# Attention with v in three pieces of 336, 352 and 336 queries across key steps, instead of 256, 256 and 512

## The chip, the cores and the metric

The kernel runs on one core of a Trainium2 chip, as one program in one launch. The metric is the device time of that core in microseconds (us); lower is better. The engines of the core work side by side, each through its own instructions in order: TensorE (PE in the profile, its weight loads PEld), VectorE (DVE), ScalarE (ACT), GpSimd (POOL) and SyncE (SP), which issues the DMAs. They meet at semaphores.

## What is computed

A transformer block of 2048 tokens of width 576, modulated by a condition vector `c`: multi-query attention of 32 heads of 18, all with one k and one v, and then a channel MLP of width 4608. Cut to the part that the change touches:

```python
def _A_ref(x, wq, wk, wv, wo):
    q = (x @ wq).reshape(B, S, H, Dh).transpose(0, 2, 1, 3)
    k = x @ wk
    v = x @ wv
    scores = jnp.einsum("bhqd,bkd->bhqk", q, k) * (Dh ** -0.5)
    p = softmax(scores, axis=-1)
    o = jnp.einsum("bhqk,bkd->bhqd", p, v)
    return o.transpose(0, 2, 1, 3).reshape(B, S, H * Dh) @ wo
```

Everything is float32; products with matrices that are used often are split into high and low parts.

## The kernel before

The program has three stages: norms, projections and the first softmax maxima; then the attention loop; then the output projection's rest and the MLP. The change is in the attention loop alone.

**Quads and key steps.** The loop goes over 32 quads (`n`): 512 queries (`TB`) of four heads at a time. For each quad the 2048 keys are taken in 16 key steps of 128 keys (`kc`). A key step makes four score products (`st_mm`, L793), one for each head: 128 keys by 512 queries, into one of four psB buffers. ACT takes the exponential of each (L795) into the tile `P` of the key step, which holds 4 x 512 columns. There are three buffers for `P`. The four products with v (`pv_mm`, L782), one for each head, then add V of these 128 keys times `P` into the quad's accumulator psC. They use 32 columns of PE's array each and stand side by side in it. psC has one buffer; when a quad is done, ACT copies it out (`O`, L613), and only then the next quad's products with v may begin.

**Maxima.** The softmax subtracts each query's maximum over the keys, and this is worked out one quad ahead. A unit (`UNITS`, eight to a quad) gives the maxima of 128 queries of two heads (`mx_mm`). For the first head of the pair there are four products of 512 keys each (tokens `m0`), for the second head two (`m1`); each goes into one of three psM buffers, and VectorE reduces it to a maximum (L815). The rest of the second head takes the two tokens `x1` and `r1`: `x1` (L803) multiplies the queries with the difference of two blocks of keys, into a psB buffer, and ACT takes its positive part (`xc`, L806); `r1` multiplies with the other block, into a psM buffer, and VectorE adds `xc` and takes the maximum in one instruction (L813).

**The order by hand.** The loop `for d in range(8 * NQT)` does two key steps each (called a double step here), `n, kd = divmod(d, 8)`. Within it the order of PE's work is a list of tokens. `MIX` is used where a unit of maxima falls on the double step (246 of 256), `PLAIN` in the last ten. `s0` and `s1` are score products on the lower and upper 64 rows of PE's array, and `m0`, `m1`, `x1`, `r1` are as above on rows 0 to 63 or 64 to 127, so that a 0 and a 1 next to each other can run side by side. `P` is a full set of four products with v over 512 queries, and `H` is half a set, over 256. With

```python
    MIX = "x1 m0 m0 s1 s0 r1 H s1 s0 m1 s0 H m0 s1 m1 s0 s1 m0 P".split()
```

the two halves are of the second key step of the double step before, and the `P` is the first key step of this one.

After the second `H`, and after the `P`, the loop calls `between`. It takes the steps of the work beside the loop: the copy and scaling of a finished quad (`post_quad`), loads of the next queries, and, from generators, the modulation products, the output projection of finished blocks (`wo_block`, L594), the second layer norm (`ln2_block`) and, on GpSimd, the splitting of the MLP's weights (`weight_parts`). The schedule is the code's order on each engine; nothing moves an instruction.

Of the kernel before, what the change touches and what calls it, by code (L numbers as in the profile page):

```python
# [14 lines left out]
S, D, H, DH, F = 2048, 576, 32, 18, 4608  # L15
NB = 4
TB = S // NB
# [3 lines left out]
NQT = NB * NQ  # L21
# [11 lines left out]
def block_kernel(ctx: ExitStack, tc, x, wqkv, wo, w1, b1, w2, b2, c, wmod, ident_in, out):  # L33
# [20 lines left out]
    def psC(): return PS["t"].tile([128, 512], F32, name="psC", bufs=1)  # L54

    open_ps("1", 3)
    def big(): return per.tile([128, 10, 512], F32R, name="big", bufs=3)
# [244 lines left out]
    def load_q(n):  # L302
        tb, qd = divmod(n, NQ)
        if n not in QST:
            new_q(n)
        q = QST[n]
        for g in range(2):
            for r in range(3):
                src = qscr[tb, r // 2, 4 * DH * qd:4 * DH * (qd + 1), :]
                src = src.rearrange("(p g d) t -> g d p t", p=2, g=2)[g]  # L310
                sy.dma_start(q[64 * g + DH * r:64 * g + DH * (r + 1)].bitcast(F32), src)
# [30 lines left out]
    def smax_fin1(n):  # L342
        m = MR[n] = pa.tile([128, 16], F32, name="mxf", bufs=2)
        mm = MX.pop(n)
        if n == 0:
            ve.tensor_reduce(m, mm, axis=AX.X, op=ALU.max)
        else:
            ve.tensor_reduce(m[:, :8], mm[:, :8, :], axis=AX.X, op=ALU.max)
            ve.tensor_reduce(m[:, 8:], mm[:, 8:, :3], axis=AX.X, op=ALU.max)

    def smax_fin2(n):
        p = psB()
        pe.transpose(p[:16, :128], MR.pop(n), ident)
        ms = pa.tile([16, 2, 128], F32R, name="ms")
        ac.activation(ms[:, 0], p[:16, :128], AF.Copy, scale=-1.0)
        ve.scalar_tensor_tensor(ms[:, 1], p[:16, :128], -1.0, ms[:, 0].bitcast(F32), op0=ALU.mult, op1=ALU.subtract)
        for g in range(2):
            for s in range(2):
                r = 64 * g + R3 + s
                sy.dma_start(QST[n][r:r + 1].rearrange("o p (t c) -> o (p t) c", c=128).bitcast(F32),  # L360
                             ms[8 * g:8 * (g + 1), s].bitcast(F32))
# [80 lines left out]
    for tb in range(NB):  # L442
# [3 lines left out]
        for i, m in enumerate((4, 0, 1, 2, 3)):  # L446
            np_ = NPART[tb][i]
# [29 lines left out]
            if tb < 2:  # L477
                for _ in range(NSTAT[tb][i]):
                    ln1_stats(*stats.popleft())
                for _ in range(NAPPLY[tb][i]):  # L480
                    b, t = applies.popleft()
# [89 lines left out]
    def ln2_block(tb):  # L571
        if "b" not in B2:
            B2["b"] = b2_scaled(load_b2())
        if tb % 2 == 0:
            YR[tb // 2] = per.tile([128, 2 * KD, TB], F32, name="yr", tag="big", bufs=3)
        for t in range(NT):
            yield from ln2_tile(tb, t)
        if tb % 2:
            R = YR[tb // 2]
            po.tensor_tensor(R[:, 5:7], R[:, 7:9], R[:, 5:7], op=ALU.subtract)  # L580
            yield
            po.tensor_tensor(R[:, 5:7], R[:, 5:7], R[:, 0:2], op=ALU.add)
            yield
# [16 lines left out]
    def wo_block(tb):  # L600
        for t in range(NT):
            for h2 in range(2):
                p = psB()
                wo_mm(tb, t, h2, p, 0, KD)
                wo_add(tb, t, h2, p)
                yield

    def post_quad(n, PV):

        tb, qd = divmod(n, NQ)  # L610
        e = po if n < NQT - 1 else ve
        O = px.tile([128, TB], F32, name="O")
        ac.activation(O, PV, AF.Copy)  # L613
        yield
        yield
        T = px.tile([128, 16, 32], F32, name="T")
        ve.transpose(T.rearrange("p a b -> p (a b)"), O)
        yield
        R = px.tile([128, 16], F32, name="R", bufs=2)
        ve.reciprocal(R, T[:, :, DH])  # L620
        e.tensor_tensor(T, T, R[:, :, None].to_broadcast([128, 16, 32]), op=ALU.mult)
        yield
        if e is po:
            yield
        ve.transpose(O, T.rearrange("p a b -> p (a b)"))
        yield
        A = ATT[tb].rearrange("p (s k) t -> p s k t", s=2)
        if qd == NQ - 1:
            os = A[:, :, KD - 1, :]
        else:  # L630
            os = px.tile([128, 2, TB], F32R, name="os")
        ac.activation(os[:, 0], O, AF.Copy)
        e.tensor_tensor(os[:, 1], O, os[:, 0].bitcast(F32), op=ALU.subtract)
        if qd < NQ - 1:
            for j in range(4):
                k, r = divmod(4 * qd + j, HC)
                sy.dma_start(A[DH * r:DH * (r + 1), :, k, :].bitcast(F32), os[32 * j:32 * j + DH].bitcast(F32))
        yield
# [8 lines left out]
    def load_w1(i, what, save=False):  # L647
        for w in what.split():
            a = 4 * OPS.index(w) if w in OPS else 28
            b = min(a + 4, 31)  # L650
            ends = W1["r"][:, a:b].bitcast(F32), w1scr[i, :, a:b]
            sy.dma_start(*(ends[::-1] if save else ends))
# [99 lines left out]


    SH = 2
    MIX = "x1 m0 m0 s1 s0 r1 H s1 s0 m1 s0 H m0 s1 m1 s0 s1 m0 P".split()
    PLAIN = "s0 s1 s0 s1 P s0 s1 s0 s1 P".split()
    P, PVt = {}, {}
    posts = []
    fill = deque([late_weights()])

    def step(q):
        if q:
            try:
                next(q[0])
            except StopIteration:
                q.popleft()

    units = {}
# [3 lines left out]
                units[8 * (n - 1) + u - SH] = (n, u)  # L772
    assert min(units) == 0 and u1 == 2 * SH

    def pv_mm(n, kc, h0, h1):

        if kc == 0 and h0 == 0:
            PVt[n] = psC()
        t = P.pop((n, kc)) if h1 == 4 else P[n, kc]
        cs = slice(128 * h0, 128 * h1)  # L780
        for j in range(4):
            pe.matmul(PVt[n][32 * j:32 * (j + 1), cs], V[:, kc, :], t[:, j, cs],  # L782
                      start=(kc == 0 and h0 == 0), stop=(kc == 15), skip_group_check=True)
        if kc == 15 and h1 == 4:
            gen = post_quad(n, PVt.pop(n))
            next(gen)
            posts.append(gen)

    def st_mm(n, kc, g, i):
        if (n, kc) not in P:  # L790
            P[n, kc] = pb.tile([128, 4, TB], F32, name="P", bufs=3)
        t = psB()
        pe.matmul(t, KS[64 * g:64 * g + 64, 128 * kc:128 * (kc + 1)], QST[n][64 * g:64 * g + 64, i, :],  # L793
                  start=True, stop=True)
        ac.activation(P[n, kc][:, 2 * i + g, :], t, AF.Exp, scale=SCALE)  # L795
# [21 lines left out]
    def between(n, kc):  # L817

        if kc == 12 and n + 1 < NQT:
            smax_fin1(n + 1)  # L820
        if kc == 13 and n + 1 < NQT:
            smax_fin2(n + 1)
        for gen in list(posts):
            if next(gen, 0) == 0:
                posts.remove(gen)
        if kc == 1 and n >= 1 and n + 2 < NQT:
            load_q(n + 2)
        if kc == 8 and n % NQ == 0 and n:
            fill.append(wo_block(n // NQ - 1))
            if n // NQ - 1 < 2:  # L830
                fill.append(ln2_block(n // NQ - 1))
        if kc % 2:
            step(fill)
        if n > 2 and kc not in (11, 12):
            step(prep)
        if kc == 8 and n == NQT - 1:
            while prep:
                step(prep)
            W1["r"] = per.tile([128, 40, 128], F32R, name="w1a", tag="big", bufs=3)
            load_w1(0, " ".join(OPS) + " tails")  # L840

    for d in range(8 * NQT):
        n, kd = divmod(d, 8)
        if kd == 0 and n % NQ == 0:
            ATT[n // NQ] = big()
        un = units.get(d)
        ns, nm, np_ = [0, 0], [0, 0], 0
        for tok in MIX if un else PLAIN:
            if tok in "PH":
                s, h0 = 2 * d + np_ // 4, np_ % 4  # L850
                np_ += 4 if tok == "P" else 2
                if s:
                    pv_mm(*divmod(s - 1, 16), h0, (np_ - 1) % 4 + 1)
                if np_ % 4 == 0:
                    between(n, s % 16)
                continue
            g = int(tok[1])
            if tok[0] == "s":
                st_mm(n, 2 * kd + ns[g] // 2, g, ns[g] % 2)
                ns[g] += 1  # L860
            else:
                mx_mm(*un, tok[0], g, nm[g])
                nm[g] += tok[0] == "m"
    pv_mm(NQT - 1, 15, 0, 4)
    while fill:
        step(fill)
    a2.__exit__(None, None, None)
# [471 lines left out]
```

## Time and profile before

| | us |
|---|---|
| three runs, median (lowest to highest) | 2322.13 (2321.21 to 2322.68) |
| the profiled execution, first to last instruction | 2317.3 |
| first to last double step with a unit of maxima, start to start | 137.7 to 1381.8 |
| busy in 150 to 1390 us: PE, DVE, ACT, POOL | 1225.69, 1142.13, 1151.64, 545.57 |

The granted TensorE clock averages 0.999 over the span. The page of the profile gives no time of the profiled execution beyond its span. A row of the groups has the line, engine, operation, tiles and shapes, the count, then the busy time, the mean length of one in ns, and the idle time of the engine just before these instructions with what ended most of it. A row of the timeline has start, length, engine, line, operation and tiles, the count of merged instructions, and in brackets the idle time before it. `x8` on a row of the products with v are eight instructions for four products.

### The profile page before, as it was taken

The numbers are of one execution on the slowest core, as the hardware profiler recorded it, in microseconds if no ns is written. First come the engines' busy times: TensorE is split into PE (matmuls) and PEld (weight loads), VectorE is DVE, ScalarE is ACT, GpSimd is POOL, SyncE is SP. The second block draws the span as 40 slices with busy tenths as digits, with TensorE's granted clock in tenths as the row PEclk, the third lists the DMA queues.
The fourth block names the chain that finished last, engine by engine and source line by source line (L and its number), as shares of the span: only waits on it lengthen the run. The fifth ranks groups of instructions, "written<-read, shape, count | busy, mean of one in ns | idle before, by whom it ended". The sixth has DMA issues, their size and how long they took to land.

```text
span 2317.3 us, 44805 instructions
## 1 busy us (share of the span) xinstructions
PE 2279.1 (98%) x16390; PEld 1417.5 (61%) x16390; DVE 1881.2 (81%) x3356; ACT 1655.6 (71%) x3166; POOL 1278.2 (55%) x1491
## 2 busy tenths in 40 slices
PE   8999999999999999999999999999999999999999
PEld 5643334454444454444444435899999988888888
DVE  6589999979999979999889993666666677878786
ACT  5568999979999979999889997444444454444443
POOL 6501534335565416656334332488888767777776
PEclk9999999999999999999999999999999999999999
DMA  6412122212222212222212222444434456666663
GB/s 224 143 62 73 50 77 78 84 45 86 73 76 70 79 50 78 76 73 80 67 60 77 79 73 85 147 150 168 163 139 174 154 171 188 181 177 181 177 180 118
DMA packets 145629, 259.93 MB, mean 112 GB/s; under 512 B 15756, under 2 KB 56588, under 8 KB 145410
## 3 DMA queue, kind: packets, MB, share of 16 engines
q1 hardware_dynamic: 145409, 257.07, 35.0%
q8 instruction: 129, 2.11, 0.4%
q14 instruction: 91, 0.74, 0.1%
HBM read 156.11 MB, written 92.01 MB: 107 GB/s over the span
## 4 chain that ended last, share of the span: by engine, by line
PE 86%; ACT 4%; POOL 2%; DVE 1%; issue 1%; DMA 0%; SPq 0%; POOLq 0%; DVEq 0%; ACTq 0%
PE psC L782 22%; PE psB L1009 16%; PE psB L793 11%; PE psM L315 10%; PE psA L1126 9%; PE psA L1095 8%; PE psB L803 4%; PE psB L594 2%; ACT P L795 2%; ACT O L613 1%; PE psA L594 1%; PE psB L152 0%; PE psB L244 0%; PE psB L199 0%; DMA bigw<-in_wo 0%
## 5 line engine op out<-in xcount | busy, mean ns | idle before, releaser
L795 ACT ACTIVATE P<-psB 128x512 f32<-128x512 f32 x2048 | 1048.1, 619 | 3.1 <-PE psB L793 2.0
L815 DVE TENSOR_REDUCE mx<-psM 128x1 f32<-128x512 f32 x1476 | 943.3, 682 | 47.7 <-PE psM L315 26.3
L782 PE MATMUL psC<-P,V 128*32 128x256 f32 (+1 forms) x6056 | 598.0, 466 | 13.3 <-ACT O L613 13.3
L793 PE MATMUL psB<-qst,KS 64*128 64x512 f32 x2048 | 597.7, 433 | 0.8 <-ACT xc L806 0.8
L315 PE MATMUL psM<-KS,qst 64*128 64x512 f32 x1722 | 596.1, 432 | 0.2
L793 PEld LDWEIGHTS psB<-qst,KS 64*128 64x128 f32 x2048 | 301.5, 184 | 169.1 <-issue 71.7
L1009 PE MATMUL psB<-ops,w1a 128*128 128x512 f32 x1512 | 391.3, 396 | 3.2 <-DVE gx L1031 2.6
L315 PEld LDWEIGHTS psM<-KS,qst 64*128 64x128 f32 x1722 | 284.4, 184 | 122.9 <-DVE mx L813 90.6
L1009 PEld LDWEIGHTS psB<-ops,w1a 128*128 128x128 f32 x1512 | 271.4, 188 | 52.0 <-DVE gx L1031 3.5
L782 PEld LDWEIGHTS psC<-P,V 128*32 128x32 f32 x6056 | 119.5, 108 | 233.4 <-issue 209.3
L1126 PE MATMUL psA<-w2s,big 128*128 128x288 f32 x1488 | 255.4, 295 | 0.0
L1126 PEld LDWEIGHTS psA<-w2s,big 128*128 128x128 f32 x1488 | 221.3, 188 | 6.6
L806 ACT ACTIVATE xc<-psB 128x512 f32<-128x512 f32 x246 | 149.0, 606 | 89.7 <-PE psM L315 75.3
L1029 ACT ACTIVATE psB<-gs 128x512 f32<-128x512 f32 x144 | 86.7, 602 | 124.8 <-DVE gs L1028 124.8
L813 DVE CUSTOM_DVE_ANT_0 xc<-psM,xc 128x512 f32<-128x512 f32 x246 | 167.2, 680 | 1.2 <-ACT xc L806 1.2
L132 POOL MEMSET qst<- 32x1024 f32 x62 | 58.7, 946 | 196.8 <-issue 71.7
L1130 DVE TENSOR_TENSOR XT<-psA,XT 128x576 f32<-128x576 f32 x152 | 113.2, 748 | 48.2 <-PE psA L1126 48.1
L803 PEld LDWEIGHTS psB<-KD,qst 64*128 64x128 f32 x246 | 45.1, 183 | 158.6 <-ACT P L795 108.7
L1033 ACT ACTIVATE big<-gx 128x512 fp32r<-128x512 f32 x72 | 45.6, 633 | 126.0 <-DVE gx L1031 126.0
L1034 POOL TENSOR_TENSOR big<-gx,big 128x512 fp32r<-128x512 f32 x72 | 96.3, 1338 | 68.6 <-ACT big L1033 68.3
L1101 DVE TENSOR_TENSOR XT<-psA,XT 128x576 f32<-128x576 f32 x170 | 125.3, 754 | 5.1 <-PE psA L1095 0.5
L803 PE MATMUL psB<-KD,qst 64*128 64x512 f32 x246 | 122.3, 497 | 0.0
(199 smaller groups left out, 3318.1 us busy)
## 6 DMA issues: line engine op xcount, KB each, us to landing
w1a<-w1scr SPq DMA_DIRECT2D x154, 256.0 KB
w1scr<-w1a SPq DMA_DIRECT2D x98, 256.0 KB
w2scr<-r SPq DMA_DIRECT2D x72, 288.0 KB
w2sum<-r SPq DMA_DIRECT2D x68, 288.0 KB
w2s<-w2sum SPq DMA_DIRECT2D x68, 288.0 KB
w2s<-w2scr SPq DMA_DIRECT2D x29, 576.0 KB
qst<-qscr SPq DMA_DIRECT2D x192, 72.0 KB
w2s<-w2scr SPq DMA_DIRECT2D x34, 288.0 KB
```

Source lines behind the costliest of these rows:

```text
L315: pe.matmul(o, QST[n][64 * g:64 * g + 64, p, 128 * qt:128 * (qt + 1)], KS[64 * g:64 * g + 64, 512 * kb:512 * (kb + 1)], start=True, stop=True)
L782: pe.matmul(PVt[n][32 * j:32 * (j + 1), cs], V[:, kc, :], t[:, j, cs], start=(kc == 0 and h0 == 0), stop=(kc == 15), skip_group_check=True)
L793: pe.matmul(t, KS[64 * g:64 * g + 64, 128 * kc:128 * (kc + 1)], QST[n][64 * g:64 * g + 64, i, :], start=True, stop=True)
L795: ac.activation(P[n, kc][:, 2 * i + g, :], t, AF.Exp, scale=SCALE)
L803: pe.matmul(t, QST[n][64 * g:64 * g + 64, p, 128 * qt:128 * (qt + 1)], KD1[64 * g:64 * g + 64, :], start=True, stop=True)
L806: ac.activation(XC[-1], t, AF.Relu)
L813: ve.tensor_tensor_reduce(c, t, c, 1.0, -3.0e38, ALU.add, ALU.max, o)
L815: ve.tensor_reduce(o, t, axis=AX.X, op=ALU.max)
L1009: pe.matmul(o, x, y, start=(first and i == 0), stop=(i == len(terms) - 1), skip_group_check=True)
L1095: pe.matmul(p[:, i, :288], x[:, ts_], W2S[k][:, y], start=(bool(first) and q == 0), stop=(q == 2), skip_group_check=True)
L1101: ve.tensor_tensor(o, p[:, :, :288], o, op=ALU.add)
L1126: pe.matmul(p[:, nn, :288], x, y, start=(q == 0), stop=(q == len(terms) - 1))
```

## The change

A double step with a unit has three pieces of products with v as before, in the same places of the token list, but of nearly equal width. A constant `CUT = 160, 336` gives the borders. The first piece takes the last 176 queries of the first key step of the double step before and the first 160 queries of its second key step. The second piece takes that key step's other 352 queries. The third takes the first 336 queries of this double step's first key step. `between` is called behind the second and the third piece, as before. In `PLAIN` the two pieces stay 512 wide, but for the rest of 176 in the first of them. The first argument in a piece counts key steps from the double step's first.

```diff
-    MIX = "x1 m0 m0 s1 s0 r1 H s1 s0 m1 s0 H m0 s1 m1 s0 s1 m0 P".split()
+    MIX = "x1 m0 m0 s1 s0 r1 P s1 s0 m1 s0 P m0 s1 m1 s0 s1 m0 P".split()
     PLAIN = "s0 s1 s0 s1 P s0 s1 s0 s1 P".split()
+    CUT = 160, 336
...
-    def pv_mm(n, kc, h0, h1):
-
-        if kc == 0 and h0 == 0:
+    def pv_mm(n, kc, c0, c1):
+
+        if kc == 0 and c0 == 0:
             PVt[n] = psC()
-        t = P.pop((n, kc)) if h1 == 4 else P[n, kc]
-        cs = slice(128 * h0, 128 * h1)
+        t = P.pop((n, kc)) if c1 == TB else P[n, kc]
+        cs = slice(c0, c1)
         for j in range(4):
             pe.matmul(PVt[n][32 * j:32 * (j + 1), cs], V[:, kc, :], t[:, j, cs],
-                      start=(kc == 0 and h0 == 0), stop=(kc == 15), skip_group_check=True)
-        if kc == 15 and h1 == 4:
+                      start=(kc == 0 and c0 == 0), stop=(kc == 15), skip_group_check=True)
+        if kc == 15 and c1 == TB:
...
-        ns, nm, np_ = [0, 0], [0, 0], 0
+        ns, nm = [0, 0], [0, 0]
+        a, b = CUT
+        if un:
+            pieces = [[(-2, b, TB), (-1, 0, a)], [(-1, a, TB)], [(0, 0, b)]]
+        else:
+            pieces = [([(-2, b, TB)] if d - 1 in units else []) + [(-1, 0, TB)], [(0, 0, TB)]]
         for tok in MIX if un else PLAIN:
-            if tok in "PH":
-                s, h0 = 2 * d + np_ // 4, np_ % 4
-                np_ += 4 if tok == "P" else 2
-                if s:
-                    pv_mm(*divmod(s - 1, 16), h0, (np_ - 1) % 4 + 1)
-                if np_ % 4 == 0:
-                    between(n, s % 16)
+            if tok == "P":
+                for s, c0, c1 in pieces.pop(0):
+                    if 2 * d + s >= 0:
+                        pv_mm(*divmod(2 * d + s, 16), c0, c1)
+                if len(pieces) < 2:
+                    between(n, 2 * kd + 1 - len(pieces))
                 continue
...
-    pv_mm(NQT - 1, 15, 0, 4)
+    pv_mm(NQT - 1, 15, 0, TB)
```

## The prediction

> **What bounds the kernel now.** I read the page first, for the stretch that the change touches and for the engines' load in it.
>
> ```profile
> PE   8999999999999999999999999999999999999999
> ...
> DVE  6589999979999979999889993666666677878786
> ACT  5568999979999979999889997444444454444443
> ...
> L795 ACT ACTIVATE P<-psB 128x512 f32<-128x512 f32 x2048 | 1048.1, 619 | 3.1 <-PE psB L793 2.0
> L815 DVE TENSOR_REDUCE mx<-psM 128x1 f32<-128x512 f32 x1476 | 943.3, 682 | 47.7 <-PE psM L315 26.3
> L782 PE MATMUL psC<-P,V 128*32 128x256 f32 (+1 forms) x6056 | 598.0, 466 | 13.3 <-ACT O L613 13.3
> ...
> L315 PEld LDWEIGHTS psM<-KS,qst 64*128 64x128 f32 x1722 | 284.4, 184 | 122.9 <-DVE mx L813 90.6
> ...
> L806 ACT ACTIVATE xc<-psB 128x512 f32<-128x512 f32 x246 | 149.0, 606 | 89.7 <-PE psM L315 75.3
> L813 DVE CUSTOM_DVE_ANT_0 xc<-psM,xc 128x512 f32<-128x512 f32 x246 | 167.2, 680 | 1.2 <-ACT xc L806 1.2
> ```
>
> In the attention loop (about slices 3 to 24 of 40) three engines are nearly full at once, so the shares don't say which one sets the pace. PE's 98% is the weakest of them: ends of matmuls are modelled, and a PE that waits with two products in flight counts as busy. Starts of weight loads show the waiting better. The list of the line that opens a double step says how many there are:
>
> ```profile
> L803 PE MATMUL psB<-KD,qst x246: 491/496/792, 137.7 to 1381.8; 64*128 64x512 f32 x123
> ```
>
> So 245 distances between first and last: (1381.8 - 137.7) / 245 = 5.08 us per double step ("step" below). In code order a step has an opening group (x1 m0 m0 s1 s0 r1), piece 1 of the products with v, a middle group (s1 s0 m1 s0), piece 2, a closing group (m0 s1 m1 s0 s1 m0) and piece 3. The timeline of three such steps, weight loads only, one row for the start of each part, and s0 and r1 of the second opening group (714.02, 714.26):
>
> ```profile
> 709.07 0.18 PEld L803 LDWEIGHTS psB<-KD,qst 64*128 64x128 f32 x1 [0.84 <-issue]
> ...
> 709.98 0.16 PEld L782 LDWEIGHTS psC<-P,V 128*32 128x32 f32 x8 [0.36 <-issue]
> ...
> 710.55 0.19 PEld L793 LDWEIGHTS psB<-qst,KS 64*128 64x128 f32 x2 [0.41 <-issue]
> ...
> 711.22 0.16 PEld L782 LDWEIGHTS psC<-P,V 128*32 128x32 f32 x8 [0.27 <-issue]
> ...
> 711.79 0.18 PEld L315 LDWEIGHTS psM<-KS,qst 64*128 64x128 f32 x1 [0.41 <-DVE mx L813]
> ...
> 712.68 0.16 PEld L782 LDWEIGHTS psC<-P,V 128*32 128x32 f32 x8 [0.26 <-issue]
> ...
> 713.68 0.18 PEld L803 LDWEIGHTS psB<-KD,qst 64*128 64x128 f32 x1 [0.84 <-ACT P L795]
> ...
> 714.02 0.18 PEld L793 LDWEIGHTS psB<-qst,KS 64*128 64x128 f32 x1
> ...
> 714.26 0.18 PEld L315 LDWEIGHTS psM<-KS,qst 64*128 64x128 f32 x1
> ...
> 714.68 0.16 PEld L782 LDWEIGHTS psC<-P,V 128*32 128x32 f32 x8 [0.24 <-issue]
> ...
> 715.25 0.19 PEld L793 LDWEIGHTS psB<-qst,KS 64*128 64x128 f32 x2 [0.41 <-issue]
> ...
> 715.92 0.16 PEld L782 LDWEIGHTS psC<-P,V 128*32 128x32 f32 x8 [0.36 <-issue]
> ...
> 716.49 0.18 PEld L315 LDWEIGHTS psM<-KS,qst 64*128 64x128 f32 x1 [0.41 <-DVE mx L813]
> ```
>
> Differences of starts: opening group 0.91 (709.07 to 709.98), piece 1 0.57, middle group 0.67, piece 2 0.57, closing group 0.89, piece 3 1.00, sum 4.61: PE's own work. In the next step the opening group takes 1.00 instead (713.68 to 714.68). The 0.41 or 0.84 idle in front of the loads behind a piece is the piece itself streaming. The row at 711.79 names L813, but the first row below shows that L813 ended at 711.55; the 90.6 us on the page are no real wait.
>
> Why 1.00? The row behind it is from VectorE's own timeline, cut at 714.2:
>
> ```profile
> 710.87 0.68 DVE L813 CUSTOM_DVE_ANT_0 xc<-psM,xc 128x512 f32<-128x512 f32 x1
> ...
> 712.32 1.89 DVE L815 TENSOR_REDUCE mx<-psM 128x1 f32<-128x512 f32 x3
> ```
>
> The x3 are the three maxima of the closing group, back to back, ending at 714.21. There are three psM buffers, and after these three come m0, m0, r1 of the next opening group: r1 takes the buffer that the last of the three frees. Its load starts at 714.26, 0.05 behind, and piece 1 follows 0.42 later, in order. That is a loop: closing group starts 711.79; first maximum 0.53 later; three maxima 1.89; 0.05; r1 0.42: **2.89 from the closing group to the next piece 1**. From there PE leads: 0.57 + 0.67 + 0.57 = 1.81 to the next closing group (716.49). Sum 4.70, against PE's own 4.61. VectorE is not short of capacity here. It is held by when the closing group starts, and r1 is held by it.
>
> **The change part by part.** *Widths.* A piece took 0.57 at 256 queries and 1.00 at 512: 0.43 per 256, or 1.68 ns per query, and 0.14 that doesn't grow. So 336 cost 0.70 and 352 cost 0.73. Piece 3 loses 0.30, piece 1 gains 0.13, piece 2 gains 0.16. The queries per step are 1024 as before, and PE's own work is 0.91 + 0.70 + 0.67 + 0.73 + 0.89 + 0.70 = 4.60.
>
> *The added group.* Piece 1 is now two groups of products (176 queries of one key step, 160 of the next), so a step has 16 instead of 12 products. The nearest row is the end of the loop, where two groups follow each other:
>
> ```profile
> 1427.36 0.16 PEld L782 LDWEIGHTS psC<-P,V 128*32 128x32 f32 x8 [0.24 <-issue]
> 1427.82 0.21 PEld L782 LDWEIGHTS psC<-P,V 128*32 128x32 f32 x2 [0.30 <-issue]
> 1428.24 0.30 PEld L782 LDWEIGHTS psC<-P,V 128*32 128x32 f32 x4 [0.22 <-issue]
> ```
>
> Each product is two loads and two passes. The second group's first loads go in at 1427.82, while the first group streams, and its second loads at 1428.24, when its own first pass begins: 0.88 from group to group at 512 queries, against 1.00 where other products follow, and 0.86 of pure streaming. The added group so costs 0.02 of its own; at most it pays the whole 0.14, and below nothing it can't go, because all queries stream as before. I take 0.03, by that one row.
>
> The Trainium skill, "TensorEngine Tiling (Array Packing)", Instruction Overhead, speaks against the change: about 60 cycles for each matmul. At the 2.4 GHz of its page "TensorE: Matmul & The Clock Gate" eight more instructions would be an estimated 0.2 us a step, if none overlapped, and 49 us over 246 steps. The rows above show groups of eight loads issued within 0.16 us and next to nothing between groups, so the sum goes without it.
>
> *The loop.* Piece 3 lies inside the 2.89, in the time in which PE waits for VectorE anyway; pieces 1 and 2 lie outside it, where VectorE waits for PE. The change moves 0.30 from the first place into the second. PE's way through the first place is now 0.89 + 0.70 + 0.91 = 2.50, and r1 still can't start before the third maximum: 2.89 stays, the wait grows from about 0.1 to about 0.4. Then 0.70 + 0.03 + 0.67 + 0.73 = 2.13. **A step that this loop sets takes 5.02 instead of 4.70.** The middle m0 of the opening group waits too (second maximum), ahead of r1, and adds nothing. What else queues behind r1 is piece 1, which feeds nothing but psC, and the middle group; ACT, whose exps wait for that, has room: eight exps back to back take 4.02, and xc 0.60, in 5.02 (row below).
>
> *Which steps.* Some steps hold more than their own parts, from the calls between the pieces, such as products for the output weights on PE and transposes on VectorE:
>
> ```profile
> L594 PE MATMUL psB<-wos,big 126*128 126x288 f32 x312 | 48.0, 303 | 0.0
> ```
>
> ```profile
> 708.99 0.70 DVE L617 STREAM_TRANSPOSE T<-O 128x512 f32<-128x512 f32 x1
> ```
>
> Of the 245 distances between L803 rows (first and last quoted above), 165 are below 5.02 and fall short of it by 43.9 us in all. The other 80 I take to hold work that already fills the wait: products between piece 3 and x1 (from 2.89 - 2.50 = 0.39 on), or VectorE's extra work. They pay only the 0.03: 2.4 us. A long step is often followed by a short one that it has relieved; averaged in pairs the 43.9 are 37.2, and I take half of the difference off, 3.4.
>
> *Quad borders.* There piece 3 waits for ACT to empty psC (the last row is the eight exps of the next step):
>
> ```profile
> 703.94 0.18 PEld L803 LDWEIGHTS psB<-KD,qst 64*128 64x128 f32 x1 [0.84 <-ACT P L795]
> ...
> 706.65 0.18 PEld L315 LDWEIGHTS psM<-KS,qst 64*128 64x128 f32 x1 [0.41 <-DVE mx L813]
> ...
> 707.40 0.62 ACT L613 ACTIVATE O<-psC 128x512 f32<-128x512 f32 x1
> ...
> 708.07 0.16 PEld L782 LDWEIGHTS psC<-P,V 128*32 128x32 f32 x8 [0.60 <-ACT O L613]
> ...
> 710.12 4.02 ACT L795 ACTIVATE P<-psB 128x512 f32<-128x512 f32 x8
> ```
>
> Due at 706.65 + 0.89 = 707.54, it comes 0.53 late. The step from x1 at 703.94 to x1 at 709.07 takes 5.13. Afterwards such a wait falls into the 0.4 that PE waits in any case, so the step takes 5.02: 31 borders by 0.11 give 3.4 back.
>
> *The rest.* The calls between the pieces stand where they stood, with the same DMAs, SP and POOL work. A tile P lives on to the next step's piece 1; the exps that need its buffer belong to the fifth s of that step, which PE issues behind piece 1, so they don't wait. Only the loop over queries changes; behind 1429 us nothing does.
>
> Sum: 43.9 + 2.4 - 3.4 - 3.4 = **39.5 us more**. The profiled span is 2317.3, and the median of the runs, 2322.13, is 4.8 above it; that part I leave as it is: 2361.6.
>
> **The rivals.** *Faster: the pieces even out ACT's supply.* ACT idles 89.7 us in front of xc, because x1 stands behind the long piece 3; 0.30 earlier x1 would end most of that. If what holds r1 at 714.26 were ACT (s0 just ahead of it waiting for a psB buffer) instead of the third maximum, the wait would shrink with piece 3, from the point where x1 comes 0.1 earlier. Short steps, now 5.02 - 43.9 / 165 = 4.75 on average, would go to 4.63 (4.60 and the group's 0.03): 165 by 0.12, 20 us less, 2302. For it speaks ACT's idle time; against it that s0's load stands at 714.02, so s0 had its buffer, and r1's, at 714.26, stands 0.05 behind the third maximum.
>
> *The added group pays its 0.14 in full.* Then the loop gives 5.13; 181 steps are short of that by 62.4 in all, the other 64 pay 9.0: with the same 3.4 twice off, about 65 more, 2387. For it: each piece alone pays 0.14. Against: the row at 1428.24.
>
> *Hidden.* VectorE's new idle time (5.02 less seven reductions of some 0.6) takes in the extra work that now lengthens steps, which I have counted in pairs only. Averaged over eight steps the shortfall is 27.2, and if the loop also had 0.1 of slack in each of the 245 steps (24.5), 2.7 would be left: 2325. For it: 80 steps are above 5.02 today; against it: most of the short ones follow each other.
>
> *It doesn't do what it says:* late buffers or later exps could stall a piece. Piece 3 needs the first four exps of its step, as before; I give this no chance of its own.
>
> **How the numbers follow.** Forecast (r1's loop, 2361.6, its own range 2340 to 2380) 0.62; full 0.14 0.12; hidden 0.09; faster 0.17. A measurement of this kernel tells about 0.2%, 4.6 us, from no change. Slower 0.62 + 0.12 = 0.74, same 0.09, faster 0.17. The range 2318 to 2388 holds the forecast, the hidden case and most of the full price, and leaves out the faster case.
>
> **What would show it.** Right: opening groups of about 1.3 (x1 to piece 1) where they are 1.00, with r1's load 0.05 behind the third maximum; 2.89 unchanged; piece 1 to middle group 0.73; psC matmuls up by 8 per step; digits of DVE and ACT lower in slices 3 to 24. Wrong: opening groups of 0.91 would mean that something else held r1; piece 1 at 0.84 the full price of the added group.

## The result and the profile after

| | before | after |
|---|---|---|
| median of four runs, us | 2322.3 (2321.21 to 2322.68) | 2356.97 (2352.93 to 2358.34) |
| ratio, 95% interval | | 1.0151 (1.0139 to 1.0163) |
| profiled execution, first to last instruction, us | 2317.3 | 2356.5 |

The change makes the kernel 34.7 us slower. Forecast were 39.5 us more (2361.6). The profiled execution of after is the slowest of its four runs (2358.34), so its own difference is larger, 39.2 us. The line that opens a double step, and the page's groups that answer to those of before (the change adds lines, so L782 is now L783, and so on up):

```profile
L804 PE MATMUL psB<-KD,qst x246: 490/494/792, 139.5 to 1419.9; 64*128 64x512 f32 x123
```

```profile
DVE  6589899978999979999879992666666677878786
ACT  5568999978999979999879999444444453434343
...
L796 ACT ACTIVATE P<-psB 128x512 f32<-128x512 f32 x2048 | 1063.8, 616 | 60.8 <-PE psB L794 59.3
L816 DVE TENSOR_REDUCE mx<-psM 128x1 f32<-128x512 f32 x1476 | 934.9, 682 | 98.1 <-PE psB L794 56.1
...
L783 PE MATMUL psC<-P,V 128*32 128x352 f32 (+4 forms) x8024 | 599.4, 393 | 9.0 <-ACT O L613 9.0
...
L807 ACT ACTIVATE xc<-psB 128x512 f32<-128x512 f32 x246 | 150.3, 611 | 65.9 <-PE psM L315 42.3
```

From first to last double step it was 1244.1 us (1381.8 - 137.7) and is 1280.4 (1419.9 - 139.5). So 36.3 of the 39.2 are in the loop, in work that has not grown: the busy time of the products with v is 599.4 against 598.0, for 8024 instructions against 6056. What has grown is idleness. ACT's exps now wait 60.8 us for scores (3.1 before), VectorE's maxima 98.1 (47.7 before), and PE waits too. Only in front of xc does ACT idle less, 65.9 us instead of 89.7; x1 now stands behind a shorter piece 3. Weight loads of one double step and the next show where, first row piece 3 of the step before:

```profile
279.58 0.16 PEld L783 LDWEIGHTS psC<-P,V 128*32 128x32 f32 x8 [0.37 <-issue]
280.29 0.18 PEld L804 LDWEIGHTS psB<-KD,qst 64*128 64x128 f32 x1 [0.55 <-ACT P L796]
...
281.20 0.18 PEld L315 LDWEIGHTS psM<-KS,qst 64*128 64x128 f32 x1 [0.30 <-DVE mx L816]
281.62 0.46 PEld L783 LDWEIGHTS psC<-P,V 128*32 128x32 f32 x16 [0.24 <-issue]
282.33 0.19 PEld L794 LDWEIGHTS psB<-qst,KS 64*128 64x128 f32 x2 [0.25 <-issue]
...
282.98 0.16 PEld L783 LDWEIGHTS psC<-P,V 128*32 128x32 f32 x8 [0.35 <-issue]
283.71 0.18 PEld L315 LDWEIGHTS psM<-KS,qst 64*128 64x128 f32 x1 [0.57 <-issue]
...
284.60 0.16 PEld L783 LDWEIGHTS psC<-P,V 128*32 128x32 f32 x8 [0.37 <-issue]
285.31 0.18 PEld L804 LDWEIGHTS psB<-KD,qst 64*128 64x128 f32 x1 [0.55 <-ACT P L796]
...
286.18 0.18 PEld L315 LDWEIGHTS psM<-KS,qst 64*128 64x128 f32 x1 [0.30 <-DVE mx L816]
286.60 0.46 PEld L783 LDWEIGHTS psC<-P,V 128*32 128x32 f32 x16 [0.24 <-issue]
...
288.70 0.18 PEld L315 LDWEIGHTS psM<-KS,qst 64*128 64x128 f32 x1 [0.57 <-issue]
```

and VectorE's timeline, cut at 286.0:

```profile
284.24 1.89 DVE L816 TENSOR_REDUCE mx<-psM 128x1 f32<-128x512 f32 x3 [0.46 <-PE psB L794]
```

The closing group starts at 283.71, its first maximum 0.53 later, three maxima take 1.89 and end at 286.13, r1's load stands 0.05 behind them, piece 1 0.42 behind that, at 286.60: 2.89 from closing group to piece 1, as before. The opening group (280.29 to 281.62) takes 1.33 instead of 1.00, piece 1 0.71, piece 2 0.73, and from closing group to closing group it is 4.99 (283.71 to 288.70). VectorE idles 0.46 before its three maxima, which is the other side of the same loop.

The median length of each part, worked out from the starts of the parts in all 244 double steps with three pieces, here for every kernel that was run, with its time (all in us). The time goes by the sum over all steps and not by a median, so the column "whole" does not put the kernels in the order of their times:

| kernel | opening | piece 1 | middle | piece 2 | closing | piece 3 | whole | time |
|---|---|---|---|---|---|---|---|---|
| before | 1.00 | 0.57 | 0.67 | 0.57 | 0.90 | 1.00 | 4.91 | 2322.3 |
| after | 1.30 | 0.71 | 0.66 | 0.73 | 0.89 | 0.70 | 5.01 | 2356.97 |
| cut_424 | 1.15 | 0.65 | 0.66 | 0.64 | 0.89 | 0.85 | 4.97 | 2334.73 |
| cut_496 | 1.03 | 0.61 | 0.66 | 0.60 | 0.90 | 0.97 | 4.90 | 2327.21 |
| short_max_thirds | 0.89 | 0.71 | 0.67 | 0.73 | 0.89 | 0.70 | 4.79 | 2296.37 |
| short_max_before | 0.89 | 0.57 | 0.66 | 0.57 | 0.89 | 1.00 | 4.79 | 2301.20 |
| r1_late_thirds | 0.67 | 0.71 | 0.90 | 0.73 | 0.97 | 0.70 | 4.88 | 2327.36 |
| r1_late_before | 0.66 | 0.57 | 0.90 | 0.57 | 1.13 | 1.00 | 4.92 | 2353.58 |
| two_max_thirds | 1.03 | 0.71 | 0.69 | 0.73 | 0.90 | 0.70 | 4.92 | 2340.14 |
| two_max_before | 0.89 | 0.57 | 0.87 | 0.57 | 0.90 | 1.00 | 4.99 | 2347.91 |
| spread_max_thirds | 1.05 | 0.71 | 0.66 | 0.73 | 0.91 | 0.70 | 4.94 | 2338.45 |
| four_psm_thirds | 1.03 | 0.71 | 0.85 | 0.73 | 1.01 | 0.70 | 5.19 | 2405.48 |
| piece3_640 | 0.89 | 0.46 | 0.74 | 0.46 | 1.01 | 1.21 | 4.93 | 2342.88 |
| piece3_552 | 0.90 | 0.54 | 0.67 | 0.54 | 0.94 | 1.07 | 4.85 | 2320.44 |

### The profile page after: what moved, and what is told of

Same layout as the page of the kernel before. It is cut to its first block, busy times and chain, and to the rows that moved or that the text cites. A ratio compares the mean times of both kernels' runs of the same rounds, so it can differ in the third digit from the quotient of the medians.

```text
span 2356.5 us, 48741 instructions
## 1 busy us (share of the span) xinstructions
PE 2322.8 (99%) x18358; PEld 1484.5 (63%) x18358; DVE 1877.6 (80%) x3356; ACT 1658.4 (70%) x3166; POOL 1276.7 (54%) x1491
## 4 chain that ended last, share of the span: by engine, by line
PE 88%; DVE 3%; POOL 2%; ACT 1%; issue 1%; DMA 0%; SPq 0%; POOLq 0%; ACTq 0%; DVEq 0%
PE psC L783 22%; PE psB L1014 17%; PE psB L794 12%; PE psM L315 11%; PE psA L1131 10%; PE psA L1100 8%; PE psB L804 4%; PE psB L594 2%; DVE mx L816 1%; ACT O L613 1%; PE psA L594 1%; PE psB L152 0%; PE psB L244 0%; DMA bigw<-in_wo 0%; PE psB L199 0%
## 5 line engine op out<-in xcount | busy, mean ns | idle before, releaser
L796 ACT ACTIVATE P<-psB 128x512 f32<-128x512 f32 x2048 | 1063.8, 616 | 60.8 <-PE psB L794 59.3
L816 DVE TENSOR_REDUCE mx<-psM 128x1 f32<-128x512 f32 x1476 | 934.9, 682 | 98.1 <-PE psB L794 56.1
L315 PE MATMUL psM<-KS,qst 64*128 64x512 f32 x1722 | 624.9, 437 | 0.5
L783 PE MATMUL psC<-P,V 128*32 128x352 f32 (+4 forms) x8024 | 599.4, 393 | 9.0 <-ACT O L613 9.0
L315 PEld LDWEIGHTS psM<-KS,qst 64*128 64x128 f32 x1722 | 292.5, 184 | 209.4 <-issue 70.9
L783 PEld LDWEIGHTS psC<-P,V 128*32 128x32 f32 x8024 | 183.5, 108 | 262.4 <-issue 230.4
L794 PEld LDWEIGHTS psB<-qst,KS 64*128 64x128 f32 x2048 | 282.9, 184 | 98.0 <-issue 60.6
L1131 PEld LDWEIGHTS psA<-w2s,big 128*128 128x128 f32 x1488 | 221.3, 188 | 6.6
L807 ACT ACTIVATE xc<-psB 128x512 f32<-128x512 f32 x246 | 150.3, 611 | 65.9 <-PE psM L315 42.3
L1100 PEld LDWEIGHTS psA<-w2s,big 128*128 128x128 f32 x816 | 115.4, 188 | 6.2
```

The costliest lines, as they stand in the source:

```text
L315: pe.matmul(o, QST[n][64 * g:64 * g + 64, p, 128 * qt:128 * (qt + 1)], KS[64 * g:64 * g + 64, 512 * kb:512 * (kb + 1)], start=True, stop=True)
L807: ac.activation(XC[-1], t, AF.Relu)
L816: ve.tensor_reduce(o, t, axis=AX.X, op=ALU.max)
L1100: pe.matmul(p[:, i, :288], x[:, ts_], W2S[k][:, y], start=(bool(first) and q == 0), stop=(q == 2), skip_group_check=True)
L1131: pe.matmul(p[:, nn, :288], x, y, start=(q == 0), stop=(q == len(terms) - 1))
```

## The experiments

**The theory** is that of the prediction: r1 waits for the psM buffer that the closing group's third maximum frees; piece 1 stands behind r1; so what is taken from piece 3 becomes waiting, and what is added to pieces 1 and 2 lengthens the loop. **Rival 1**: the added group of products costs the time. **Rival 2**: the longer pieces bring the scores, and with them ACT, late. The kernel before ran at 2320.7 to 2321.3 beside these.

### The wait taken away

`short_max_thirds` is the changed kernel with a quarter of VectorE's reading in the closing group's three maxima:

```diff
+            late = kb >= 2 if g == 0 else kb == 1
-            ve.tensor_reduce(o, t, axis=AX.X, op=ALU.max)
+            ve.tensor_reduce(o, t[:, :128] if late else t, axis=AX.X, op=ALU.max)
...
-        ac.activation(P[n, kc][:, 2 * i + g, :], t, AF.Exp, scale=SCALE)
+        ac.activation(P[n, kc][:, 2 * i + g, :], t, AF.Exp, scale=SCALE / 64)
```

> The changed kernel, but VectorE's maximum of the three products of the closing group reads only the first 128 of 512 columns; the exponent's scale is a 64th so that nothing overflows (the output is another, the instructions are the same in number and, but for these maxima, in size). Theory (r1 waits for the third maximum): the three maxima take about 0.7 instead of 1.89, r1 finds its buffer free, the opening group falls from 1.30 to 0.91 and a plain step from 5.01 to 4.6 to 4.7, the time to 2295 to 2315. Rival 1 (added instructions): 2357, unchanged. Rival 2 (the scores and ACT are late behind longer pieces): the opening group keeps most of its 1.30, the time stays above 2345.

Measured: 2296.37 us, ratio to before 0.989 (0.9874 to 0.9907), 61 us less than the changed kernel. VectorE's timeline and the weight loads of one closing group and the piece 1 after it:

```profile
285.13 0.78 DVE L817 TENSOR_REDUCE mx<-psM 128x1 f32<-128x128 f32 x3 [0.47 <-PE psM L315]
```

```profile
284.59 0.18 PEld L315 LDWEIGHTS psM<-KS,qst 64*128 64x128 f32 x1 [0.57 <-DVE mx L814]
...
285.49 0.16 PEld L783 LDWEIGHTS psC<-P,V 128*32 128x32 f32 x8 [0.36 <-issue]
286.19 0.18 PEld L804 LDWEIGHTS psB<-KD,qst 64*128 64x128 f32 x1 [0.55 <-ACT P L796]
...
287.08 0.46 PEld L783 LDWEIGHTS psC<-P,V 128*32 128x32 f32 x16 [0.36 <-issue]
```

The maxima take 0.78 instead of 1.89, the opening group 0.89, and closing group to piece 1 is 2.49: PE's own 2.50 of the prediction, and not 2.89. Sixteen products and the long pieces 1 and 2 are all there. Rivals 1 and 2 both fall as the cause of the 34.7 us. Shorter maxima also give VectorE less work in all; but VectorE was not short of time, since it idles 0.46 before the three maxima in the changed kernel (row above), and `r1_late_thirds` below gains 30 us with all maxima whole.

`short_max_before` is the kernel before with the same two edits.

> The kernel before (256, 256, 512) with the same shortened maxima of the closing group (first 128 of 512 columns) and the exponent's scale a 64th; the output is another. Theory (the widths cost time only through r1's wait): with the wait gone in both, the two sets of widths take the same time within 5 us, 2291 to 2301 against 2296.4. If equal pieces were worth something by themselves (ACT fed more evenly), this one is slower than 2301; if the added group cost something by itself, it is faster than 2291.

Measured: 2301.2, ratio 0.9916 (0.9902 to 0.993). Within 5 us of the other, as expected, and if anything slower: the two intervals overlap only a little. The mean closing group, waits at quad borders included, is 0.97 here and 0.94 in `short_max_thirds`, which over 244 steps is 6.6 us, and the page of each says what for:

```profile
L782 PE MATMUL psC<-P,V 128*32 128x256 f32 (+1 forms) x6056 | 598.0, 466 | 14.0 <-ACT O L613 14.0
```

```profile
L783 PE MATMUL psC<-P,V 128*32 128x352 f32 (+4 forms) x8024 | 599.5, 393 | 8.9 <-ACT O L613 8.9
```

So equal pieces seem to have a small gain of their own, 4.8 us between the two medians. The emptying of psC is waited for less (14.0 us down to 8.9), as I read it because the closing group stands later behind the scores that feed ACT; no run tests that reason. Beside r1's wait the gain is not to be seen.

### The widths, with sixteen products kept

```diff
-    CUT = 160, 336
+    CUT = 212, 424
```

> The changed kernel with the borders at 212 and 424, so pieces of 300 (88 and 212), 300 and 424. Sixteen products a step, as in the changed kernel. Theory: loop 2.89 + 0.67 + 0.645 + 0.645 = 4.85 in steps without other work; over the steps the kernel before had, 9 to 20 us more than it, 2331 to 2342. Rival 1 (added instructions): as the changed kernel, 2357. Rival 2 (length of the pieces, in proportion: 88 of 176 queries moved): half of the 35, 2340; this run alone does not tell it from the theory.

```diff
-    CUT = 160, 336
+    CUT = 240, 496
```

> The changed kernel with the borders at 240 and 496, so pieces of 256 (16 and 240), 272 and 496: nearly the widths of the kernel before, but sixteen products a step. Theory: loop 4.73 at most, 1 to 9 us above the kernel before, 2323 to 2331, with piece 1 at 0.57 to 0.62. Rival 1 (each added instruction pays about 60 cycles or the group its 0.14): 35 to 50 us above the kernel before, 2357 to 2372, piece 1 at 0.71.

Measured: 2334.73 (ratio 1.0061, 1.0044 to 1.0077) and 2327.21 (1.0027, 1.0016 to 1.0037). Both are where the theory put them; rival 1 had 2357 and more for both. The opening group follows the widths, 1.30, 1.15, 1.03, while pieces 1 and 2 grow by what the formula of the prediction says. The two times alone do not tell the theory from rival 2, which would also put the cost in proportion to the widths; the shortened maxima do. `cut_496` still pays something for the added group: piece 1 of 16 and 240 queries takes 0.61, a single group of 256 takes 0.57.

### r1 moved behind piece 1

In the changed kernel, and in the same way in the kernel before, whose first two pieces are H:

```diff
-    MIX = "x1 m0 m0 s1 s0 r1 P s1 s0 m1 s0 P m0 s1 m1 s0 s1 m0 P".split()
+    MIX = "x1 m0 m0 s1 P s0 r1 s1 s0 m1 s0 P m0 s1 m1 s0 s1 m0 P".split()
```

> The changed kernel (336, 352, 336) with r1 moved behind piece 1: opening group x1 m0 m0 s1, middle group s0 r1 s1 s0 m1 s0. Nothing else differs. Theory (piece 1 is held because r1 in front of it waits for VectorE's third maximum): piece 1 and most of the middle group no longer stand behind r1, the loop from closing group to closing group is 2.42 + 0.05 + r1 and the rest of the middle group 0.9 + piece 2 0.73 = 4.1, below PE's own 4.60, so a step without other work takes about 4.62 (now 5.01) and the time falls by 45 to 60 us, to 2297 to 2312, below the kernel before. Rival 1 (the eight added instructions per step cost the time): no change, 2357, within 5. Rival 2 (the two longer pieces delay the scores, ACT starves in front of the middle group): the order of r1 changes that little, at most 10 us, 2347 to 2357.

> The kernel before (256, 256, 512) with r1 moved behind piece 1 in the same way. Theory: the loop that sets 4.70 in its plain steps goes, PE's own 4.61 stays; the 165 steps that are now under 5.02 stand 25 us above 4.61 in all, so the time falls by 12 to 28 us, to 2294 to 2310. Rivals 1 and 2 have nothing to say against the kernel before being as fast as PE allows: 2322, within 5. Beside the changed kernel with r1 moved, the theory also says that the widths then matter little: the two within 8 us of each other.

Measured: 2327.36 (1.0028, 1.0017 to 1.004) and 2353.58 (1.014, 1.0125 to 1.0156). The first gains 30 us on the changed kernel but does not reach the kernel before; the second was expected faster and is 32 us slower than the kernel before. r1's wait is gone in both (opening group 0.67, piece 1 0.57 or 0.71 behind it; the middle group, where r1 now stands, takes 0.90, and the two together are within 0.01 of the kernels with shortened maxima). What came instead is in the closing group of the second:

```profile
292.57 0.18 PEld L315 LDWEIGHTS psM<-KS,qst 64*128 64x128 f32 x1 [0.41 <-DVE mx L813]
...
293.27 0.18 PEld L793 LDWEIGHTS psB<-qst,KS 64*128 64x128 f32 x1 [0.31 <-ACT P L795]
...
293.70 0.16 PEld L782 LDWEIGHTS psC<-P,V 128*32 128x32 f32 x8 [0.24 <-issue]
```

The closing group's last s waits for a psB buffer, that is for an exp. With r1 its partner s0 had moved behind piece 1 too, so, as I read it, ACT had one score less early in the step and was late by the end of it; no run moves r1 without a score. That was not in my expectation: the edit moves one product of VectorE's and one of ACT's, and by this row it is ACT's that holds PE. As a test of r1 alone this pair is weak.

### Two maxima ahead of r1's buffer

Three ways were tried to let r1 need the second maximum instead of the third: one maximum moved from the closing into the middle group, in both kernels (with H for the first two P in the kernel before), and one moved from the opening into the middle group in the changed one.

```diff
-    MIX = "x1 m0 m0 s1 s0 r1 P s1 s0 m1 s0 P m0 s1 m1 s0 s1 m0 P".split()
+    MIX = "x1 m0 m0 s1 s0 r1 P s0 s1 m0 m1 P m0 s1 s0 m1 s0 s1 P".split()
```

> The changed kernel with one maximum moved out of the closing group: middle group s0 s1 m0 m1, closing group m0 s1 s0 m1 s0 s1, opening group as it was, so two maxima of the closing group stand ahead of r1's buffer instead of three. Theory: r1 may start when the second ends, about 1.87 behind the closing group's start, before PE gets to it (0.89 + 0.70 + 0.36 = 1.95): no wait for VectorE; ACT's four exps of the closing group can hold the opening s0 by up to 0.2; a plain step 4.60 to 4.75, 2300 to 2325. Rival 1: 2357. Rival 2: the closing group's fourth score makes ACT later still, 2357 or above.

> The kernel before (256, 256, 512) with the same order of groups, two maxima in the closing group. Theory: PE's own 4.61 sets the plain steps, where r1's wait of 0.1 made 4.70; ACT has 0.3 more behind piece 3 than in the run beside it; 2297 to 2315. Rival: ACT's order, not VectorE's third maximum, sets 4.70; then 2322 or above, as r1 behind piece 1 gave.

```diff
-    MIX = "x1 m0 m0 s1 s0 r1 P s1 s0 m1 s0 P m0 s1 m1 s0 s1 m0 P".split()
+    MIX = "x1 m0 s1 s0 s0 r1 P m0 m1 s0 s1 P m0 s1 m1 s0 s1 m0 P".split()
```

> The changed kernel (336, 352, 336) with one m0 moved from the opening group into the middle group and one s0 the other way: x1 m0 s1 s0 s0 r1, piece 1, m0 m1 s0 s1, piece 2, m0 s1 m1 s0 s1 m0, piece 3. Two psM products in the opening group, two in the middle, three in the closing group. Theory: r1 now takes the buffer of the second maximum of the closing group, free 1.87 behind its start; PE comes to it at 1.95. No wait for VectorE there, and the middle group's two find theirs free as well (at 2.4 and 3.0, wanted at 3.3). Left are the opening group's second s0, which may wait up to 0.2 for ACT, and the closing group's third product, which wants the middle group's second maximum within 0.05. Plain steps 4.62 to 4.80, 2303 to 2325, about the kernel before or below; opening group 0.9 to 1.1. If r1's place in the order and not its buffer held PE, the opening group stays 1.30 and the time 2357.

Measured: 2340.14 (1.0081, 1.0066 to 1.0096), 2347.91 (1.0113, 1.0098 to 1.0128) and 2338.45 (1.0071, 1.0057 to 1.0085). The mechanism answered as expected: the opening group of the changed kernel falls from 1.30 to 1.03 and 1.05, that of the kernel before to 0.89. The times did not, all three expectations were too low. What is left above 0.89 in the two orders of the changed kernel is the opening group's last s0, which waits for an exp: its load stands within 0.07 behind the end of one in 208 of 244 steps in `two_max_thirds` (one of them below) and in 181 in `spread_max_thirds`:

```profile
288.10 0.18 PEld L794 LDWEIGHTS psB<-qst,KS 64*128 64x128 f32 x1 [0.29 <-ACT P L796]
```

In `two_max_before` the wait stands one group further on, in the middle group's m1:

```profile
292.56 0.16 PEld L782 LDWEIGHTS psC<-P,V 128*32 128x32 f32 x8 [0.36 <-issue]
293.12 0.19 PEld L793 LDWEIGHTS psB<-qst,KS 64*128 64x128 f32 x2 [0.41 <-issue]
...
293.57 0.18 PEld L315 LDWEIGHTS psM<-KS,qst 64*128 64x128 f32 x1 [0.15 <-DVE mx L815]
294.00 0.16 PEld L782 LDWEIGHTS psC<-P,V 128*32 128x32 f32 x8 [0.25 <-issue]
```

```profile
292.23 1.29 DVE L815 TENSOR_REDUCE mx<-psM 128x1 f32<-128x512 f32 x2 [0.50 <-PE psM L315]
```

It takes the buffer of the opening group's second m0, whose maximum ends at 292.23 + 1.29 = 293.52, 0.05 ahead of the load. The middle group takes 0.87 instead of 0.67. With three psM buffers every product with psM takes the buffer of the one three before it; here the order took the wait from r1 and gave it to m1.

### Another buffer

`four_psm_thirds` gives psM a fourth buffer and takes one from psB:

```diff
-    def psM(): return PS["t"].tile([128, 512], F32, name="psM", bufs=3)
+    def psM(): return PS["t"].tile([128, 512], F32, name="psM", bufs=4)
...
-    open_ps("2", 4)
+    open_ps("2", 3)
```

> The changed kernel with four psM buffers and three psB buffers (instead of three and four) in the attention loop. Theory: r1 now needs the buffer that the second maximum frees, 1.87 behind the closing group's start, before PE reaches it at 1.95; no wait of r1 for VectorE is left. What the smaller psB then costs is ACT's: the opening group's s0 waits for the exp of the closing group's last s, by 0.15 to 0.3, a plain step 4.75 to 4.95, 2315 to 2345. Rival (r1's place, not its buffer, holds PE): r1's load still 0.05 behind the third maximum and 2357.

Measured: 2405.48 (1.0362, 1.0348 to 1.0377), far above what was expected. r1 is freed: in the median its load now stands 0.22 before the end of the closing group's third maximum; before and after it never stands ahead of it. The price of three psB buffers was sized too low. The waits of the score products' loads for exps head its list of waits:

```profile
PEld psB L794 <- ACT P L796: 190.2, 636, 1.0
```

### The other direction

```diff
-            pieces = [[(-2, b, TB), (-1, 0, a)], [(-1, a, TB)], [(0, 0, b)]]
+            pieces = [[(-1, 0, 192)], [(-1, 192, 384)], [(-1, 384, TB), (0, 0, TB)]]
+            if kd == 0:
+                pieces = [[(-1, 0, 256)], [(-1, 256, TB)], [(0, 0, TB)]]
```

> The other direction: pieces of 192, 192 and 640 (the second key step's last 128 queries stand in front of the next first key step's 512), but 256, 256 and 512 in the first double step of a quad. Sixteen products a step. Theory: loop 2.89 + 0.67 + 0.46 + 0.46 = 4.48, below PE's own 4.61, so r1's wait goes (opening group 0.89); if nothing else took its place 2297 to 2310. What can take its place is ACT, as with r1 behind piece 1: the third s of the closing group waits for the exp of the second s0, and comes sooner behind the opening group, by 0.2; then about 4.7 and 2315 to 2325. Rival 1 (added instructions): above the kernel before, 2335 and more.

The second run has 236 and 472 in place of 192 and 384.

> Pieces of 236, 236 and 552 (256, 256, 512 in the first double step of a quad). Between the two limits found so far: r1's loop, 4.70 at piece 3 of 512 and falling with it by 1.67 ns per query to 4.63, and the loop by which the closing group's third s waits for ACT, 4.785 at 640 and rising with piece 3, so 4.64 at 552. Theory: plain steps of 4.62 to 4.66, some 107 of them 0.05 shorter than before: 3 to 9 us less than the kernel before, 2312 to 2318. If one of the two loops has another slope, the same as the kernel before or slower.

Measured: 2342.88 (1.0095, 1.008 to 1.011) and 2320.44 (0.9997, 0.9988 to 1.0006). With 640 the opening group is 0.89, so r1's wait is gone as the theory has it, but the closing group takes 1.01 and the middle group 0.74; the row at the closing group's third s says why:

```profile
292.86 0.18 PEld L794 LDWEIGHTS psB<-qst,KS 64*128 64x128 f32 x1 [0.28 <-ACT P L796]
```

It is ACT's side again, and it cost more than expected. The 552 between the two limits is no faster than 512, and its 3 to 9 us did not come. Averaged over the steps, its opening group is 0.04 shorter than that of the kernel before (0.95 against 0.99), and its closing group 0.03 longer (1.02 against 0.99): what the one wait gave up, the other took. Of the kernels that keep the maxima whole, none is faster than the kernel before.

## Why the prediction was right

**r1's loop.** Right, and shown: 2.89 before and after, gone when the maxima were shortened. Counted over the 245 double steps that follow another, r1's load stands within 0.07 behind the maximum that frees its buffer in 173 before and in 203 after. The plain step went from 4.70 to 4.99 to 5.01, for a forecast 5.02.

**PE's own work.** 4.60 was forecast for the new widths without a wait; the shortened maxima gave 2.49 for the part that was put at 2.50, and 0.71, 0.66 and 0.73 for the rest, 4.59.

**The added group.** I took 0.03, from one place where two groups follow each other. Piece 1 of 176 and 160 takes 0.707 in the median where 0.70 were worked out for one group of 336, so about 0.01 at most. The upper end 0.14, and with it the rival of 2387, is out. For widths like these the rule of the Trainium skill of about 60 cycles for each matmul ("TensorEngine Tiling (Array Packing)", Instruction Overhead) does not show in the trace: eight more instructions cost about 0.01 us at most. With 16 queries in the first group (`cut_496`) the split costs 0.04; whether that is this rule, no run here tells.

**Which steps.** The size of this term was off. The 165 short steps got 30.0 us longer, not 43.9 - 3.4 = 40.5. The other 80 got 6.4 longer (4.6 without a quad border, 1.8 with one), not 2.4 - 3.4. Together 36.3 against 39.5. So the closeness of the sum is in part luck: 10.5 too much in one term and 7.4 too little in the other nearly cancel.

A large part of the first miss lies at the borders. I sized the border by one step of 5.13, and counted the short step behind it (4.57 in most quads) as if it went to 5.02. It is the pair that counts: 5.22 + 4.57 = 9.79 in a plain quad of before, 5.37 + 4.64 = 10.01 after, or 0.22 where the terms give 0.34. Over the 30 borders among these steps (I had counted 31) the pairs grew by 3.8 us in all, where the terms give 6.8; the 3.4 taken off for pairs already hold some of that difference. Whole quads that hold nothing else went from 4.79 per step to 5.00; quads with layer norms beside them went from 4.82 to 4.99 up to 4.98 to 5.17, by 0.1 to 0.2. There, as I read it, some of the new waiting fell into VectorE's extra work, which I had taken into account only by half a difference between pairs; no run separates this. Why the 50 long steps without a border grew by 0.09 each and not by 0.03 is not worked out here.

**Quad borders.** That the wait for psC would be hidden was right: piece 3 still comes 0.37 late,

```profile
307.98 0.16 PEld L783 LDWEIGHTS psC<-P,V 128*32 128x32 f32 x8 [0.37 <-issue]
308.71 0.18 PEld L315 LDWEIGHTS psM<-KS,qst 64*128 64x128 f32 x1 [0.57 <-issue]
...
309.97 0.16 PEld L783 LDWEIGHTS psC<-P,V 128*32 128x32 f32 x8 [0.73 <-ACT O L613]
```

(due at 308.71 + 0.89 = 309.60), and the pair of steps takes 10.01, twice the plain 5.00.

**The rivals.** That equal pieces feed ACT better was not empty: the waits for psC fell from 13.3 to 9.0 us, and the two kernels with shortened maxima differ by 4.8 us in favour of equal pieces. But that is about a seventh of the 34.7, and on the other side of the sum. That ACT held r1 at 714.26 is out: shorter maxima alone ended the wait. In the runs here ACT held PE longer than before where pieces 1 and 2 were shortened, a score product was moved or a psB buffer was taken away. Some of the change was hidden (the 10.5 us above, in part), far from all.

## What to carry to other kernels

Where an engine works in code order, ask of each instruction that can wait what stands behind it, and cut the work ahead of it only if nothing else still has to end first. A piece of work that covers a wait is not free to move: taken from the place where PE waited for VectorE to a place where VectorE waits for PE, the same 0.30 us was lost in full in every plain step. Before a gap is evened out, take the suspected wait away by making its cause shorter (here the maxima read a quarter). Done in both kernels, this showed what the wait was worth, 61 us in the changed kernel and 20 in the kernel before, and what the evening out is worth by itself, about 5.

## What the runs showed that was not expected

The three engines hold each other closely: every order, width or buffering tried here that freed r1 from the third maximum while the maxima stayed whole met another wait, of PE for an exp (`r1_late_before`, `two_max_thirds`, `piece3_640`, `four_psm_thirds`) or of a later product for another maximum (`two_max_before`), and none came out ahead of the kernel before. A fourth psM buffer for one psB buffer cost 48.5 us on top of the change (2405.48 against 2356.97). Two groups of products with v of the same shape follow each other with no visible gap at 160 queries in the second (0.707 for both, where 0.70 is worked out for one group of 336), while a piece has 0.14 that does not grow with its width in front of products of another shape (0.57 at 256 queries, 1.00 at 512).
